# An attention and FFN kernel: a range check, two casts and a set of V loads take other places in the first two chunks

## The chip, the core and the metric

The kernel runs on one core of a Trainium2 chip. The metric is the device time of one execution in microseconds (us); less is better. The engines are TensorE (PE in the profile, with PEld for its weight loads), VectorE (DVE), ScalarE (ACT), GpSimd (POOL) and SyncE (SP). ACT, POOL and SP also issue DMAs. Each engine runs its instructions in the order in which the program gives them.

## The reference

Causal attention with a decay bias over 8 batches, 8 heads, 576 positions and head size 64, and behind it an FFN with RMS norm on the 4608 tokens:

```python
scores = scale * np.matmul(q, k.transpose(0, 1, 3, 2))
cum = np.cumsum(np.maximum(s, 0.0), axis=-1)
bias = -(cum[:, :, :, None] - cum[:, :, None, :])
scores = np.where(causal, -1000000000.0, scores + np.minimum(bias, 0.0))
attn = softmax(scores)                      # max subtracted, 1e-9 added to the sum
x = np.matmul(attn, v)                      # heads side by side: 4608 x 512
xn = x / np.sqrt(np.mean(x * x, axis=-1, keepdims=True) + 1e-06) * rms_g
g = xn @ w_gate                             # 512 x 1536
out = (g * sigmoid(g) * (xn @ w_val)) @ w_out
```

## The kernel before

**Attention by blocks.** Each batch has five blocks of positions (four of 128, one of 64). For a batch b the kernel does:

- load K and Q in float32 into `kq32` (w = 0 is K, w = 1 is Q; a main part with four row groups, and a tail), and cast them to bf16 into `kqn`, a row group at a time (`cast`, lines 139 and 141, and `cast_x`, line 149). `kqn` has two places, b % 2;
- transpose them into `kqT`. Batches 0 and 1 do it on PE (`t_step`, lines 184 to 192, and `tail_step`, lines 200 to 209); for batches 2 and 3 PE transposes K, and five DMAs of SP, c0 to c4, transpose Q (`kq_dma`, line 171); later batches use DMAs for both;
- S(b, kb, g), `s_step`: the scores of key block kb and four heads (g is 0 or 1; for kb = 4 all eight heads at once), matmuls at line 250, exponentials on ACT at line 274, and the causal mask on POOL at line 283 (`mask`);
- AV(b, qb, g), `av_step`: the value step of query block qb, matmuls at lines 300 and 306 with V in `v_sb`, and on DVE the reciprocal of the sums (line 313) and the product (line 315). After g = 1 come the sum of squares (DVE line 325 or ACT line 321) and, on POOL, its scale `al_all` (lines 328 and 331);
- `x_scale` on DVE (line 338), and a transpose into `xnT`, the input of the FFN: for batch 0 and for block 3 of batch 1 on PE (`xt_step`, line 357, copied at line 364 or 366), for the others by a DMA of SP (line 348).

V comes by DMAs that POOL issues, five per batch (`load_v`, line 175).

**The range check.** The kernel's fast path holds only for inputs within a range, so the largest magnitudes of Q and K are kept. `check_mag` (line 369, one DVE instruction of 128x2560) clears the signs into `mag`, and two `check_max` (line 375, 128x1280 each) take the running maximum into `acc`. It runs for K and Q of every batch.

**The order of work.** The program fixes the order by hand. A first part, written out instruction by instruction (lines 773 to 884), does nearly all of batch 0's attention. Then come nine FFN chunks of 512 tokens (`ffn`): 12 pairs of gate and value products (lines 668 and 677; T is ACT's tanh at line 671, U and Ht are DVE's products at lines 680 and 673), and then the output product in four blocks (line 690, copied by ACT at line 695, stored by SP at line 697). The matmuls of a chunk are cut by 36 calls of `step`, the slots; slots 1 to 36 lie in the first chunk, 37 to 72 in the second. A slot hands out the work of the coming batches: at most one entry of each side queue whose condition holds, then one score step, or value steps and transposes. `phase()` is the slot within its chunk, and slots with `bare` set skip the queue of V loads and the queue of POOL:

```python
bare = bare or chunk[0] == 0 and 30 <= phase() <= 33
if slot[0] % 2 and not bare:
    run_side(v_side)
if not bare:
    run_side(pool_side)
run_side(dve_side)
```

`later` puts functions into such a queue, due a number of slots from now; `early` does the same, and also keeps them to the first 23 slots of a chunk. `casts(b)` fills POOL's queue with the casts of batch b: five of Q, the mark `over(1)`, five of K, the mark `over(0)`. The mark `over(1)` lets Q's transposing DMAs start two slots later (at most one every second slot) and sets the loads of the next batch's Q four slots later. The mark `over(0)` lets K's transposes on PE start two slots later. A value step of batch 2 or above waits eight slots after the mark that V of its batch has been issued.

In the first chunk batch 0's last value step is in slot 10, batch 1's steps AV(1,2,1) and AV(1,3,1) are in slots 28 and 30, S(1,4) in slot 31, x_scale(1,2) and x_scale(1,3) in slots 31 and 33, and the PE transpose of block (1,3), which the second chunk needs, in slot 34. With the conditions of before, Q of batch 2 is cast by POOL in slots 24 to 28, V of batch 2 is loaded in slots 27, 29, 35, 37 and 39, `over(1)` is in slot 29, and K of batch 2 is cast in slots 34 to 38.

For the start of batch 1, ACT casts four row groups of its K in slots 1 to 4, POOL the tail in slot 1; DVE casts two row groups of its Q in slots 3 and 4, and POOL the other two and the tail in slots 4 to 6.

Of the kernel before, what the change touches and what calls it, by code (L numbers as in the profile page):

```python
# [26 lines left out]
def kernel(  # L27
# [12 lines left out]
    nc = tc.nc  # L40
# [63 lines left out]
    def psF16():  # L104
        return pp.tile([128, 8, 128], BF16, name="psF16", tag="F", bufs=4)
# [13 lines left out]
    def psT32():  # L119
        return pp.tile([128, 512], FP32, name="psT32", tag="T", bufs=1)  # L120
# [14 lines left out]
    def cast(eng, b, w, r0, r1, h0=0, h1=H):  # L135
        o = kqn[:, b % 2, w, r0:r1, h0:h1, :]
        i = kq32[:, w].rearrange("p h (r d) -> p r h d", d=D)[:, r0:r1, h0:h1, :]
        if eng is nc.scalar:
            eng.activation(out=o, in_=i, func=AF.Copy)
        else:  # L140
            eng.tensor_copy(out=o, in_=i)
# [52 lines left out]
    def tail_step(b):  # L194
        pT = psT()
        nw = 2 if b < XB else 1
        for w in range(nw):
            for hp in range(HP):
                i = w * HP + hp
                nc.tensor.matmul(  # L200
                    pT[:, i, :], lhsT=kqn[:, b % 2, w, 4, 2 * hp:2 * hp + 2, :],
                    rhs=ident_bf, is_transpose=True, start=(i == 0), stop=(i == nw * HP - 1))
        dst, src = kqTn[:, b % 2, 0, :, 512:576], pT[:, 0:HP, 0:64]
        if b == 0:
            nc.vector.tensor_copy(out=dst, in_=src)
        else:
            nc.scalar.activation(out=dst, in_=src, func=AF.Copy)
        if nw == 2:
            nc.vector.tensor_copy(out=kqTn[:, b % 2, 1, :, 512:576], in_=pT[:, HP:8, 0:64])
# [125 lines left out]
    def x_scale(b, qb):  # L335
        n = rows(qb)
        col = b * NSC + qb
        nc.vector.scalar_tensor_tensor(  # L338
            out=xs_sb[0:n, (b * NSC + qb) % NX, :], in0=x_sb[0:n, (b * NSC + qb) % NX, :],
            scalar=al_all[0:n, col:col + 1], in1=g_row[0:n], op0=ALU.mult, op1=ALU.mult)  # L340
# [32 lines left out]
    def check_max(i):  # L373
        sl = slice(i * 1280, (i + 1) * 1280)
        nc.vector.tensor_tensor(out=acc[:, sl], in0=acc[:, sl], in1=mag[:, sl], op=ALU.max)  # L375
# [27 lines left out]
    def run_side(queue):  # L403
        if queue and queue[0][0]():
            queue.pop(0)[1]()
            return True
        return False
# [21 lines left out]
    def phase():  # L429

        return slot[0] - first[0]
# [14 lines left out]
    def casts(b):  # L446

        def key(c):  # L450
            load_k(b, c)
            done["K", b, c] = slot[0]
            if c == NSC - 1:
                check(b)

        def over(w):
            done["cast", b, w] = slot[0]
            if b + 1 < B and (w == 1 or b + 1 < KB):
                loads(b + 1, w, early, 4)
            if w == 1:  # L460
                x_seq.extend((b, ww, c) for c in range(NSC) for ww in ((1, 0) if b >= KB else (1,)))
            else:
                done["cast", b] = slot[0]
                check(b)

        def free(w):
            return ready(0, "check", b - 2, w) and (
                ready(0, "T", b - 2) if w == 0 and b < KB + 2 else
                b < XB + 2 or ready(4, "X", b - 2, w, 4))
        if b >= KB:  # L470
            pool_side.extend((lambda: free(0) and slot[0] % 2 == 0, lambda c=c: key(c)) for c in range(NSC))
        fns = [(1, lambda r=r: cast_x(nc.gpsimd, b, 1, r)) for r in range(NSC)]
        fns += [(1, lambda: over(1))]
        if b < KB:
            fns += [(0, lambda r=r: cast(nc.gpsimd, b, 0, r, r + 1)) for r in range(NSC)]
            fns += [(0, lambda: over(0))]
        pool_side.extend((lambda w=w: ready(7, "raw", b, w) and free(w), f) for w, f in fns)

# [3 lines left out]

    def after_av(b):
        if b + 2 < B:
            (early if b else later)(v_side, 6 if b else 16, [
                lambda r=r: load_v(b + 2, r) for r in range(NSC)]
                + [lambda: done.__setitem__(("V", b + 2), slot[0])])

# [24 lines left out]
    def do_av(key, ps=None, act=False):  # L513
        b, qb, g = key
        act = act or b > 1 or b == 1 and qb > 1
        av_step(b, qb, g, ps, act)
        done["AV", b, qb, g] = slot[0]
        last["AV"] = slot[0]
        if b > 0 and g == 1:
            last["AVT"] = slot[0]  # L520
        if qb == 4 and g == 1:
            after_av(b)

    def do_xt(key, pX=None):
        b, qb = key
        xt_step(b, qb, pX)
        done["XT", b, qb] = slot[0]
        last["T"] = slot[0]
# [13 lines left out]
    def can_s():  # L542
        if not s_seq or not slot_free():
            return False
        b, kb, g = s_seq[0]
        if b == 1 and (phase() < 24 and phase() % 2 == 0 or kb == 4 and at("AV", 1, 3, 1) > slot[0]):
            return False
        due = SLOTS * ((b * S + kb * 128) // DM) - (26 if b == 1 else 18 if b < 4 else 14)
        if slot[0] - last["S"] < (4 if slot[0] < due - 24 else 3 if slot[0] < due else 2):
            return False  # L550
        if b >= XB:
            return all(ready(5, "X", b, 1, c) for c in (kb, min(kb + 1, 4))) and (
                ready(5, "X", b, 0, kb) if b >= KB else ready(3, "T", b) if kb >= 3 else
                all(ready(3, "T", b, hp, 0) for hp in (2 * g, 2 * g + 1)))
        if kb >= 3 and not ready(3, "T", b):
            return False
        if kb == 4:
            return True
        return all(ready(3, "T", b, 2 * g + j, w) for j in (0, 1) for w in (0, 1))
# [39 lines left out]
    def step(bare=False):  # L599

        slot[0] += 1
        while pending:
            pending.pop(0)()
        moved = False
        if scaled[0] < len(x_list):
            b, qb = x_list[scaled[0]]
            if ready(3, "AV", b, qb, 1):
                x_scale(b, qb)
                scaled[0] += 1
                if not by_pe(b, qb):  # L610
                    assert xt_seq[0] == (b, qb)
                    xt_dma(*xt_seq.pop(0))
                    done["XT", b, qb] = slot[0] + 4
                    moved = True
        run_side(act_side)
        if not moved and x_seq and slot[0] - last["X"] >= 2:
            b, w, c = x_seq[0]
            if (ready(2, "cast", b, 1) and ready(1, "S", b - 2, 4, 0)
                    and (w == 1 or ready(7, "K", b, c))):
                x_seq.pop(0)  # L620
                kq_dma(b, w, c)
                done["X", b, w, c] = last["X"] = slot[0]
                if b >= KB and (w, c) == (0, NSC - 1) and b + 2 < B:
                    casts(b + 2)
        bare = bare or chunk[0] == 0 and 30 <= phase() <= 33
        if slot[0] % 2 and not bare:
            run_side(v_side)
        if not bare:
            run_side(pool_side)
        run_side(dve_side)  # L630
        if can_s():
            pending.append(do_s(s_seq.pop(0)))
            if t_seq and t_seq[0][0] == 1 and can_t():
                do_t(t_seq.pop(0))
            return
        n = 0
        if can_xt():
            do_xt(xt_seq.pop(0))
            n += 1
        if can_av():  # L640
            do_av(av_seq.pop(0))
            n += 1
        if n < 2 and t_seq and can_t():
            do_t(t_seq.pop(0))
# [126 lines left out]
    with tc.manual_schedule():  # L771
# [31 lines left out]
        def pairF():  # L803
            return (psF(), psF())

        def s_first(kb, g, pair=None):
            do_s((0, kb, g), pair)()
# [31 lines left out]
        do_t((0, 2, 1), pT=psT(), dve=True)  # L839
        do_t((0, 3, 1), pT=psF16(), dve=True)  # L840
        do_av((0, 0, 0))
        s_first(0, 1, pairF())
        do_av((0, 1, 0), psT32())
        s_first(1, 1)
        tail_step(0)
        done["T", 0] = 0
        load_v(0, 4)
        do_av((0, 2, 0))
# [28 lines left out]
        do_xt((0, 2), psF16())  # L877
        warm(2)
        x_scale(0, 3)
        do_xt((0, 3), psF16())  # L880
        check_mag(0, 1)
        check_max(0)
        check_max(1)
        done["check", 0, 1] = 0

        def done_cast(w):
            done["cast", 1, w] = slot[0]
        later(act_side, 1, [lambda r=r: cast(ACT, 1, 0, r, r + 1) for r in range(4)])
        later(pool_side, 1, [lambda: cast(POOL, 1, 0, 4, 5)])
        later(pool_side, 3, [lambda: done_cast(0)])  # L890
        later(pool_side, 4, [lambda: cast(POOL, 1, 1, 2, 3),
# [207 lines left out]
```

## Time and profile before

| | us |
|---|---|
| median of 3 runs | 376.06 (375.62 to 376.51) |
| the profiled execution | 374.85 |
| its span, from the first to the last instruction | 373.2 |
| PE busy | 347.1 |
| DVE busy | 279.6 |
| ACT busy | 240.0 |
| POOL busy | 175.2 |

The mean granted clock of PE is 0.988. A line of the profile in order of time gives the start, the length, the engine, the line of the kernel, the operation, what it writes and reads, and how many instructions were merged; in brackets stand the engine's idle time ahead of it and what ended that idle time. `kq` stands for `kq32`. The first FFN matmul starts at 31.85, that of the second chunk at 76.10, and that of the third at 115.28.

### The profile page before, as it was taken

The numbers are of one execution on the slowest core, as the hardware profiler recorded it, in microseconds if no ns is written. First come the engines' busy times: TensorE is split into PE (matmuls) and PEld (weight loads), VectorE is DVE, ScalarE is ACT, GpSimd is POOL, SyncE is SP. The second block draws the span as 40 slices with busy tenths as digits, with TensorE's granted clock in tenths as the row PEclk, the third lists the DMA queues.
The fourth block names the chain that finished last, engine by engine and source line by source line (L and its number), as shares of the span: only waits on it lengthen the run. The fifth ranks groups of instructions, "written<-read, shape, count | busy, mean of one in ns | idle before, by whom it ended". The sixth has DMA issues, their size and how long they took to land. (4 is left out here: it accounts for less than half of the span.)

```text
span 373.2 us, 6936 instructions
## 1 busy us (share of the span) xinstructions
PE 347.1 (93%) x2356; PEld 161.4 (43%) x2356; DVE 279.6 (75%) x525; ACT 240.0 (64%) x626; POOL 175.2 (47%) x277
## 2 busy tenths in 40 slices
PE   1777899899999999899999999999999999999993
PEld 1443444454444444444444444444444444444441
DVE  6778988589887878788889897795488548837730
ACT  3787787547877597776778776777677644323321
POOL 5866734974846565779856825523322310000000
PEclk9879999999999999999999999999999999999998
DMA  7999999799997599959999997973310230020012
GB/s 228 192 206 262 148 208 210 122 201 222 127 204 104 52 200 161 159 56 204 147 166 223 139 118 151 122 56 44 99 23 14 44 105 3 0 84 31 0 42 78
DMA packets 125626, 46.22 MB, mean 124 GB/s; under 512 B 104912, under 2 KB 120784, under 8 KB 125584
## 3 DMA queue, kind: packets, MB, share of 16 engines
q0 software_dynamic: 59920, 11.80, 43.9%
q1 hardware_dynamic: 53040, 24.33, 34.7%
q10 hardware_dynamic: 12624, 9.59, 10.2%
q8 instruction: 20, 0.33, 0.4%
q14 instruction: 22, 0.18, 0.2%
HBM read 38.16 MB, written 9.44 MB: 128 GB/s over the span
## 5 line engine op out<-in xcount | busy, mean ns | idle before, releaser
L274 ACT ACTIVATE E<-psS,biasK 128x256 bf16<-128x256 f32 (+3 forms) x352 | 115.1, 416 | 19.7 <-PE psS L250 18.0
L668 PE MATMUL psF<-xnT,wg_sb 128*128 128x512 bf16 x432 | 111.1, 379 | 1.9 <-DMA xnT<-xs_sb 0.8
L677 PE MATMUL psF<-xnT,wv_sb 128*128 128x512 bf16 x432 | 111.1, 379 | 0.1
L690 PE MATMUL psF<-wout_sb,Ht 128*128 128x512 bf16 x432 | 102.3, 379 | 0.0
L283 POOL TENSOR_SCALAR_AFFINE_SELECT E<-E 128x512 bf16<-128x512 bf16 x72 | 51.9, 721 | 92.8 <-ACT E L274 92.0
L671 ACT ACTIVATE T<-psF 128x512 f32<-128x512 f32 x108 | 64.4, 598 | 41.5 <-PE psF L668 38.3
L680 DVE SCALAR_TENSOR_TENSOR U<-T,psF 128x512 bf16<-128x512 f32 x108 | 73.6, 682 | 21.8 <-ACT T L671 21.8
L673 DVE TENSOR_TENSOR Ht<-U,psF 128x512 bf16<-128x512 bf16 x99 | 67.7, 684 | 7.5 <-PE psS L250 0.5
L668 PEld LDWEIGHTS <-wg_sb 128*128 128x128 bf16 x432 | 38.7, 98 | 46.3 <-issue 7.5
L677 PEld LDWEIGHTS <-wv_sb 128*128 128x128 bf16 x432 | 38.6, 98 | 42.8 <-issue 4.6
L690 PEld LDWEIGHTS <-Ht 128*128 128x128 bf16 x432 | 38.7, 98 | 42.0 <-issue 2.3
L338 DVE SCALAR_TENSOR_TENSOR xs_sb<-x_sb,al_all,g_row 128x512 bf16<-128x512 bf16 (+1 forms) x40 | 32.4, 810 | 16.6 <-POOL al_all L331 15.0
L695 ACT ACTIVATE osb<-psF 128x512 f32<-128x512 f32 x36 | 21.4, 595 | 33.7 <-PE psF L690 29.3
L321 ACT ACTIVATE xs_sb<-x_sb 128x512 bf16<-128x512 bf16 (+1 forms) x36 | 22.9, 640 | 21.3 <-DVE x_sb L315 21.2
L175 POOL DMA_DIRECT2D v_sb<-in_v_dram x40 | 35.3, 883 | 0.4 <-issue 0.3
L375 DVE TENSOR_TENSOR acc<-acc,mag 128x1280 bf16<-128x1280 bf16 x32 | 29.5, 936 | 0.4
L250 PE MATMUL psS<-kqT 64*128 64x256 bf16 (+2 forms) x304 | 26.6, 260 | 1.4 <-ACT E L274 1.2
L306 PEld LDWEIGHTS <-E 128*128 128x128 bf16 x320 | 22.5, 99 | 12.1 <-POOL E L283 2.2
L328 POOL TENSOR_SCALAR al_all<-ss_all 128x1 f32<-128x1 f32 (+1 forms) x40 | 11.3, 282 | 27.6 <-ACT xs_sb L321 21.5
L300 PEld LDWEIGHTS <-E 128*128 128x128 bf16 x256 | 20.7, 99 | 8.0 <-DVE x_sb L315 0.8
L331 POOL TENSOR_TENSOR al_all<-al_all,mhalf 128x1 f32<-128x1 f32 (+1 forms) x40 | 22.6, 565 | 3.3
L250 PEld LDWEIGHTS <-kqT 64*128 64x128 bf16 x320 | 10.5, 96 | 29.9 <-issue 28.5
(94 smaller groups left out, 279.7 us busy)
## 6 DMA issues: line engine op xcount, KB each, us to landing
out_dram<-osb SPq DMA_DIRECT2D x36, 256.0 KB, 2.3
kq<-in_q_dram ACTq DMA_DIRECT2D x6, 1024.0 KB, 9.5
v_sb<-in_v_dram POOLq DMA_DIRECT2D x32, 128.0 KB, 7.2
kq<-in_k_dram ACTq DMA_DIRECT2D x2, 1024.0 KB, 10.6
kqn<-in_k_dram POOLq DMA_DIRECT2D x16, 128.0 KB, 4.9
wg_sb<-in_moe_w_gate_dram POOLq DMA_DIRECT2D x2, 768.0 KB, 7.3
wv_sb<-in_moe_w_val_dram POOLq DMA_DIRECT2D x2, 768.0 KB, 10.1
wout_sb<-in_moe_w_out_dram POOLq DMA_DIRECT2D x1, 1536.0 KB, 14.1
```

The source lines that it names most:

```text
L175: nc.gpsimd.dma_start(out=v_sb[0:n, b % 2, c, :, 0:64], in_=v[b, :, c * 128:c * 128 + n, :].rearrange("h p d -> p h d"))
L250: nc.tensor.matmul(pair[par][:, j * W:j * W + M], lhsT=kT, rhs=qT, start=(j == 0), stop=(j == nj - 1))
L274: nc.scalar.activation(out=eo, in_=ei, func=AF.Exp, scale=0.125, bias=biasK[:, kb, bh:bh + 1])
L283: nc.gpsimd.affine_select(out=Ev[:, :, 0:nq], in_=Ev[:, :, 0:nq], pattern=[[0, nh], [1, nq]], compare_op=ALU.is_ge, fill=0.0, base=0, chan ...
L338: nc.vector.scalar_tensor_tensor(out=xs_sb[0:n, (b * NSC + qb) % NX, :], in0=x_sb[0:n, (b * NSC + qb) % NX, :], scalar=al_all[0:n, col:col ...
L375: nc.vector.tensor_tensor(out=acc[:, sl], in0=acc[:, sl], in1=mag[:, sl], op=ALU.max)
L668: nc.tensor.matmul(Gp, lhsT=wg_sb[:, cc, fs], rhs=xnT[:, cc, x0:x0 + DM], start=(cc == 0), stop=(cc == CC - 1))
L671: nc.scalar.activation(out=T, in_=Gp, func=AF.Tanh, scale=0.5)
L673: nc.vector.tensor_tensor(out=Ht[:, fb - 1, :], in0=pend[0], in1=pend[1], op=ALU.mult)
L677: nc.tensor.matmul(Vp, lhsT=wv_sb[:, cc, fs], rhs=xnT[:, cc, x0:x0 + DM], start=(cc == 0), stop=(cc == CC - 1))
L680: nc.vector.scalar_tensor_tensor(out=U, in0=T, scalar=1.0, in1=Gp, op0=ALU.add, op1=ALU.mult)
L690: nc.tensor.matmul(Op, lhsT=Ht[:, fb, tb * 128:(tb + 1) * 128], rhs=wout_sb[:, fb, :], start=(fb == 0), stop=(fb == FB - 1))
```

## The change

Five edits, all in the first two chunks or ahead of them:

- the check of batch 0's Q (three DVE instructions) stood at the end of the first part; it is now cut up among the value steps of batch 0 there: `check_mag` behind AV(0,0,0), one `check_max` behind AV(0,1,0), the other behind the tail's transposes;
- two of the four K casts of batch 1 go from ACT (slots 3 and 4) to DVE, ahead of the last transpose of the first part;
- V of batch 2 is due 24 slots after batch 0's last value step instead of 16;
- the slots that skip the queues of V and POOL are 29 to 33 of the first chunk, instead of 30 to 33;
- the first of the K casts of batch 2 goes from POOL's queue to DVE, in slot 33.

```diff
@@ casts(b)
-            fns += [(0, lambda r=r: cast(nc.gpsimd, b, 0, r, r + 1)) for r in range(NSC)]
+            fns += [(0, lambda r=r: cast(nc.gpsimd, b, 0, r, r + 1)) for r in range(b == 2, NSC)]
@@ after_av(b)
-            (early if b else later)(v_side, 6 if b else 16, [
+            (early if b else later)(v_side, 6 if b else 24, [
@@ step()
-        bare = bare or chunk[0] == 0 and 30 <= phase() <= 33
+        bare = bare or chunk[0] == 0 and 29 <= phase() <= 33
...
         run_side(dve_side)
+        if slot[0] == 33:
+            cast(nc.vector, 2, 0, 0, 1)
@@ the first part
         do_av((0, 0, 0))
+        check_mag(0, 1)
         s_first(0, 1, pairF())
         do_av((0, 1, 0), psT32())
+        check_max(0)
         s_first(1, 1)
         tail_step(0)
+        check_max(1)
         done["T", 0] = 0
...
         x_scale(0, 3)
+        cast(DVE, 1, 0, 2, 3)
+        cast(DVE, 1, 0, 3, 4)
         do_xt((0, 3), psF16())
-        check_mag(0, 1)
-        check_max(0)
-        check_max(1)
         done["check", 0, 1] = 0
...
-        later(act_side, 1, [lambda r=r: cast(ACT, 1, 0, r, r + 1) for r in range(4)])
+        later(act_side, 1, [lambda r=r: cast(ACT, 1, 0, r, r + 1) for r in range(2)])
```

## The prediction

> **What bounds the kernel now.** I read the page first: TensorE (PE) carries the span.
>
> ```profile
> PE 347.1 (93%) x2356; PEld 161.4 (43%) x2356; DVE 279.6 (75%) x525; ACT 240.0 (64%) x626; POOL 175.2 (47%) x277
> ```
>
> So only PE's holes can give time. I listed PE in order of time for every idle gap. Before the first FFN matmul (31.85) PE waits for others all the time; after it four holes over 0.4 remain in front of the closing stage: 1.14, 0.48, 1.50, and 0.78 at 154.84 (an xnT transfer, which no edit touches). The first three:
>
> ```profile
> 36.50 0.33 PE L184 MATMUL psT<-ident_bf,kqn 128*128 128x128 bf16 x3
> 37.97 0.23 PE L184 MATMUL psT<-ident_bf,kqn 128*128 128x128 bf16 x1 [1.14 <-ACT kqn L139]
> ...
> 40.80 0.23 PE L184 MATMUL psT<-ident_bf,kqn 128*128 128x128 bf16 x1 [0.48 <-POOL kqn L141]
> ...
> 73.90 0.40 PE L357 MATMUL psT<-ident_bf,xs_sb 128*128 128x128 bf16 x4 [1.50 <-DVE xs_sb L338]
> ```
>
> Then DVE in order of time, for where the check of Q goes and what it leaves (last bracket: idle before, and its releaser):
>
> ```profile
> 17.15 0.42 DVE L315 TENSOR_TENSOR x_sb<-psAV,rZ 128x256 bf16<-128x256 f32 x1
> 18.06 0.18 DVE L313 RECIPROCAL rZ<-psT 128x4 f32<-128x4 f32 x1 [0.49 <-PE psT L306]
> ...
> 19.90 0.29 DVE L205 COPY kqT<-psT 128x256 bf16<-128x256 bf16 x1 [1.20 <-PE psT L200]
> ...
> 22.53 1.17 DVE L325 SCALAR_TENSOR_TENSOR xs_sb<-x_sb 128x512 bf16<-128x512 bf16 x1
> ...
> 30.63 1.47 DVE L369 TENSOR_SCALAR mag<-kqn 128x2560 uint16<-128x2560 uint16 x1
> 32.14 1.97 DVE L375 TENSOR_TENSOR acc<-acc,mag 128x1280 bf16<-128x1280 bf16 x2
> ```
>
> ACT and POOL around the first two holes: a K cast of ACT sits ahead of the eight exponentials of S(0,4), POOL's mask waits for those, and the Q casts that PE wants wait for the mask.
>
> ```profile
> 35.13 0.62 ACT L139 ACTIVATE kqn<-kq 128x512 bf16<-128x512 f32 x1
> 35.66 1.74 ACT L274 ACTIVATE E<-psS,biasK 128x64 bf16<-128x64 f32 x8
> 37.23 0.69 ACT L139 ACTIVATE kqn<-kq 128x512 bf16<-128x512 f32 x1
> ```
>
> ```profile
> 37.47 0.66 POOL L283 TENSOR_SCALAR_AFFINE_SELECT E<-E 128x512 bf16<-128x512 bf16 x1 [3.21 <-ACT E L274]
> 38.09 1.18 POOL L141 CAST kqn<-kq 128x512 bf16<-128x512 f32 x1
> 39.22 0.90 POOL L175 DMA_DIRECT2D v_sb<-in_v_dram  x1
> 40.12 1.78 POOL L141 CAST kqn<-kq 128x512 bf16<-128x512 f32 x2
> ...
> 70.03 0.19 POOL L328 TENSOR_SCALAR al_all<-ss_all 128x1 f32<-128x1 f32 x1
> 70.30 0.56 POOL L331 TENSOR_TENSOR al_all<-al_all,mhalf 128x1 f32<-128x1 f32 x1
> 70.82 0.95 POOL L175 DMA_DIRECT2D v_sb<-in_v_dram  x1
> 71.84 0.18 POOL L328 TENSOR_SCALAR al_all<-ss_all 128x1 f32<-128x1 f32 x1
> 72.11 0.57 POOL L331 TENSOR_TENSOR al_all<-al_all,mhalf 128x1 f32<-128x1 f32 x1
> ```
>
> The last lines are the third hole: the scale of block (1,3) stands behind a V load's issue.
>
> **A, the check between the value steps.** Three DVE instructions come into 17.57 to 22.53, where DVE idles 0.49 + 1.20 + 0.87 = 2.56 us. Alone they take 0.82 each (median of 16 and of 32), 2.46 in all, but the order is fixed. The first reads Q's tail, cast by POOL until 17.77, so it runs 17.83 to 18.65; behind it the reciprocal of AV(0,1,0) starts at 18.65 instead of 18.06, its product ends 0.56 late, and the tail transposes, which want its PSUM tile, start 0.56 late (19.41). The first max fills their 1.01 us. The second stands ahead of AV(0,2,0)'s reciprocal: after the tail copies (20.95) it ends at 21.8, that product near 22.4, AV(0,0,1)'s near 23.1, and the square (1.17) near 24.3 instead of 23.71: 0.55 late. POOL's scale of block (0,0), both last masks and the other three scales follow without a gap to spare, and so do the four transposes to xnT and the first FFN matmul. With the durations seen beside POOL work (1.11 for the mag at 37.70, 1.32 for a max at 40.11) it is 1.4. I take +0.8, since a mask (0.63) meets both maxes. At the old place nothing returns: the check held U(0) back 0.53 (34.04 against T's end 33.51), but PE's buffers had 0.8 to 1.4 us of slack there.
>
> The mag at 30.63 took 1.47, beside POOL's issue at 30.71, against 0.82 alone. The Trainium skill ("SBUF — State Buffer", section "Who interferes with whom") says that a DVE tensor_scalar in a two-port mode, or one with two SBUF inputs against a POOL instruction that reads, locks a shared port pair, and whoever comes second waits fully. By it each max waits out its mask and A is about +0.85; without it +0.55, and the whole sum -1.35 instead of -1.1.
>
> **B, two K casts from ACT to DVE.** DVE runs them (0.42 each) from x_scale(0,3)'s end, 30.71, where the check was. K landed at 23.88 + 5.5 = 29.4; both move with A, so the data is there 1.3 us early. If it were not, U(0) would wait, with the slack above. ACT loses 0.62 and 0.69: the exponentials start right after T(1) (35.24) and end at 36.88 instead of 37.40, and the 1.14 hole closes. But the next wait is the second hole's: POOL's mask and Q casts start 0.52 earlier, so the Q cast that PE waits for ends at 40.2 instead of 40.73, and PE, 1.14 early, waits there. Gain 0.52, not 1.62; 0.25 if DVE's mag of K again holds POOL (the 1.18 cast), 1.0 if it no longer does. I take -0.5.
>
> **C, POOL clear of V.** V of batch 2 moves from slots 27, 29, 35, 37, 39 to 35, 37, 39, 41, 43. Without the first two issues (0.95 each) Q's casts end near 69.0, block (1,2)'s scale runs 69.1 to 69.9, and block (1,3)'s starts when ACT's square is read (70.06): 0.19 + 0.56, then x_scale 0.75, at 71.7. PE is free for its transpose at 72.40: the 1.50 goes, or all but 0.2 if rows beside other work hold (0.80 for L328, 1.13 for x_scale). I take -1.4. Next late would be block (1,2)'s transfer to xnT: issued near 70.7, 3.6 to land (the row of before), 74.3; the next chunk then begins at 74.7. If it lands like the slowest nearby (4.6), 0.6 comes back.
>
> **Edits that go together at nothing.** The K cast on DVE in slot 33 (0.42) lies in DVE's idle 0.49 and 1.54 after x_scale(1,3); uncovered it delays an xnT copy that has 1.35 to spare. POOL then casts four rows in slots 35 to 38, and K of batch 2 is marked in slot 39 as before, so its transposes start in slot 41 as before. AV(2,0,0) goes from slot 51 to 54, since V is marked in 45 instead of 41: the same matmuls later in a busy PE. The load of Q's tail for batch 4 would fall on slot 60, where such loads are barred until the next chunk, and slips from 59 to 73; its casts slip only from 79 to 80.
>
> One move has a price: slot 29 is now barred to POOL's queue, so the mark "Q of batch 2 cast" waits until 34, and its five transposing DMAs go from slots 32 to 40 to slots 36 to 44, behind an output store. The second (c1) is issued near 77.2 instead of 74.97, and S(2,0,0) needs it at 85.85 - 1.4 = 84.4. Landings were 3.0 and 5.8 for the first two, and for the three issued beside the 1 MB load of Q (77.25):
>
> ```profile
> DMA to landing us min/median/max: 9.3/9.4/9.7
> ```
>
> Beside Q's load of batch 5, c0 and c1 landed in 6.7 and 5.4. I take 7, as those start with little queued like here: 84.2, just in time. Bounds 0 and +2.3.
>
> **Sum:** +0.8 - 0.5 - 1.4 = -1.1 on the profiled 374.85 (span 373.2 and 1.65 around it). That execution lies 1.21 under the median 376.06; on the median, 375.0.
>
> **Rivals.** *1. Q's transposes of batch 2 arrive late (slower).* In-order PE stops at S(2,0,0). For it: three of five landings above are 9.3 or more, when V and Q's load ran too, as they now do. Against: batch 5's. At 9.4, c1 lands at 86.6, 2.2 too late: -1.1 + 2.2 = +1.1, 377.2. It costs from a landing of 7.2 us on; the sign turns at 8.3, and at 9.05 the kernel is slower by 0.2%. The Trainium skill ("DMA: Bandwidth & Descriptors", section "Queues, rings and completion order") says that each DMA engine serves its queues in turn, packet by packet; by it three busy queues (SP, ACT, POOL's V) stretch c1 as they did at 77 to 81, and the trace agrees with 9.4 there against 5.4 with two. Chance 0.2.
>
> *2. The check is dearer and POOL stays the bound.* A +1.4 and B -0.25 (contention rows), C -1.3: -0.15, 375.9. For it: DVE leaves hardly a gap after 21.86. Chance 0.2.
>
> *3. Everything hides well.* A +0.55, B -1.0, C -1.5: -1.95, 374.1. For it: POOL is idle 17.77 to 19.12, when the mag runs. Chance 0.15.
>
> **Numbers.** Forecast, -1.1 and no late transfer: 0.45, faster. Rival 3 is faster, rival 2 the same, rival 1 slower in 0.15 and the same in 0.05. Faster by over 0.2% (0.75 us, about what a measurement of this kernel can tell from no change) 0.60, within it 0.25, slower 0.15. The range goes from 373.6 (rival 3, with the next chunk's holes of 0.38 at 93.03 and 0.17 at 101.12 closed too) to 377.0 (rival 1 at a landing of 9.2).
>
> **What would show it.** Right: the first FFN matmul 0.8 later; the 1.14 hole gone, a wait for POOL's Q cast near 40 of about 1 us; no hole ahead of block (1,3)'s transpose, with al_all of (1,3) right behind ACT's square; V's issues after it. Wrong: a first FFN matmul no later or over 1.4 later; a hole in front of S(2,0,0) waiting for kqT; one at the next chunk's first matmul waiting for xnT.

## The result: slower by half a per cent, and the profile after

| | median us (lowest to highest, runs) |
|---|---|
| before | 375.86 (375.19 to 377.09, 13) |
| changed | 377.65 (376.20 to 380.44, 13) |
| ratio, 95% interval | 1.0055 (1.0038 to 1.0071) |

The forecast was 375.0, faster; the change lies outside the range, on the side of rival 1 (377.2). Its profiled execution took 380.44 with a span of 378.8 and is the slowest of its 13 runs: PE's granted clock was 0.54 from 33 to 36, which cost chunk 1 about 1.7. A second profile of the same kernel (span 375.2) does not have this dip, and the profile of run 5, whose first part is that of before, has it (0.55). So where sizes are compared below, that second profile is used too. It is the fastest of its six runs (376.93 to 379.95), so it shows the loss at its small end.

PE in order of time, in the changed kernel; the lines answer to the three holes of before:

```profile
40.71 0.33 PE L184 MATMUL psT<-ident_bf,kqn 128*128 128x128 bf16 x3
42.59 0.23 PE L184 MATMUL psT<-ident_bf,kqn 128*128 128x128 bf16 x1 [1.54 <-POOL kqn L141]
...
74.03 0.39 PE L357 MATMUL psT<-ident_bf,xs_sb 128*128 128x128 bf16 x4
...
85.01 1.03 PE L679 MATMUL psF<-xnT,wv_sb 128*128 128x512 bf16 x4
88.44 0.39 PE L250 MATMUL psS<-kqT 64*128 64x256 bf16 x4 [2.40 <-DMA kqT<-kqn]
```

The holes of 1.14 and 0.48 have become one of 1.54. The hole of 1.50 ahead of block (1,3)'s transpose is gone. A new one of 2.40 stands ahead of S(2,0,0), which waits for a transposing DMA. POOL, in order of time, shows why the third hole went: both scales now come ahead of V's issues.

```profile
70.85 0.19 POOL L328 TENSOR_SCALAR al_all<-ss_all 128x1 f32<-128x1 f32 x1
71.13 0.55 POOL L331 TENSOR_TENSOR al_all<-al_all,mhalf 128x1 f32<-128x1 f32 x1
71.93 0.58 POOL L328 TENSOR_SCALAR al_all<-ss_all 128x1 f32<-128x1 f32 x1 [0.26 <-ACT xs_sb L321]
72.60 0.55 POOL L331 TENSOR_TENSOR al_all<-al_all,mhalf 128x1 f32<-128x1 f32 x1
73.56 0.89 POOL L283 TENSOR_SCALAR_AFFINE_SELECT E<-E 128x512 bf16<-128x512 bf16 x1 [0.41 <-ACT E L274]
74.40 0.95 POOL L175 DMA_DIRECT2D v_sb<-in_v_dram  x1
75.36 1.17 POOL L141 CAST kqn<-kq 128x512 bf16<-128x512 f32 x2
76.47 0.89 POOL L175 DMA_DIRECT2D v_sb<-in_v_dram  x1
```

The issues of SP and ACT, in order of time, show what the first two transposes (c0, c1) now run beside: V's two issues above, and the 1 MB load of Q, issued 0.09 behind c0.

```profile
77.28 5.05 SPq L171 DMA_TRANSPOSE kqT<-kqn  x3
77.37 0.40 ACTq L125 DMA_DIRECT2D kq<-in_q_dram  x1
```

And the landing of c0 and c1, and who waited for them (view of the transposes' line, issues from 77 to 80):

```profile
L171 SPq DMA_TRANSPOSE kqT<-kqn x2: 1430/1734/2037, 77.3 to 78.8; - x2
...
  PE psS L250: 2.4, 1
...
DMA to landing us min/median/max: 9.5/9.5/9.6
```

Before, they were issued at 72.96 and 74.97, ahead of the same load (77.25), and landed in 3.0 and 5.8. Issues in order of time, before (at 77.16 start the other three transposes, those that landed in 9.3 to 9.7):

```profile
72.96 1.23 SPq L171 DMA_TRANSPOSE kqT<-kqn  x1
...
74.26 0.95 POOL L175 DMA_DIRECT2D v_sb<-in_v_dram  x1
...
74.97 1.22 SPq L171 DMA_TRANSPOSE kqT<-kqn  x1
...
76.33 0.89 POOL L175 DMA_DIRECT2D v_sb<-in_v_dram  x1
...
77.16 4.65 SPq L171 DMA_TRANSPOSE kqT<-kqn  x3
77.25 0.39 ACTq L125 DMA_DIRECT2D kq<-in_q_dram  x1
```

Two of V's loads are issued in slots 35 and 37 in both kernels, 74.26 and 76.33 here and 74.40 and 76.47 after. What is new for c0 and c1 is their own later time, beside the load of Q and behind those two.

A chunk is measured here from its first FFN matmul to the next chunk's; in these rows the work of PE in a chunk hardly changes (38.6 to 38.9 busy in chunk 2), so a longer chunk is a chunk with holes.

| kernel | first FFN matmul | chunk 1 | chunk 2 | chunks 3 and 4 |
|---|---|---|---|---|
| before | 31.85 | 44.25 | 39.18 | 77.95 |
| changed | 32.21 | 44.01 | 43.10 | 78.80 |
| changed, second profile | 32.49 | 42.33 | 41.55 | 78.22 |

Chunk 1 gave 1.92 and chunk 2 took 2.37 back in the second profile, 0.64 was lost ahead of chunk 1 and 0.27 behind chunk 2. By chunk 5's start that is +1.36; the spans differ by 2.0, and the rest lies in the closing stage, whose length differed by some 0.6 between executions of kernels that were edited nowhere near it.

### The profile page after: what moved, and what is told of

Its sections match the earlier page's. It is cut to its first block, busy times and chain, and to the rows that moved or that the text cites. A ratio compares the mean times of both kernels' runs of the same rounds, so it can differ in the third digit from the quotient of the medians.

```text
span 378.8 us, 6937 instructions
## 1 busy us (share of the span) xinstructions
PE 348.8 (92%) x2356; PEld 161.8 (43%) x2356; DVE 280.3 (74%) x528; ACT 238.8 (63%) x624; POOL 175.8 (46%) x276
## 5 line engine op out<-in xcount | busy, mean ns | idle before, releaser
L283 POOL TENSOR_SCALAR_AFFINE_SELECT E<-E 128x512 bf16<-128x512 bf16 x72 | 54.4, 756 | 94.6 <-ACT E L274 94.0
L670 PEld LDWEIGHTS <-wg_sb 128*128 128x128 bf16 x432 | 38.9, 98 | 47.3 <-issue 9.0
L679 PEld LDWEIGHTS <-wv_sb 128*128 128x128 bf16 x432 | 38.9, 98 | 43.6 <-issue 5.7
L375 DVE TENSOR_TENSOR acc<-acc,mag 128x1280 bf16<-128x1280 bf16 x32 | 27.9, 884 | 0.3
## 6 DMA issues: line engine op xcount, KB each, us to landing
v_sb<-in_v_dram POOLq DMA_DIRECT2D x32, 128.0 KB, 10.2
```

What stands on the lines that cost most here:

```text
L283: nc.gpsimd.affine_select(out=Ev[:, :, 0:nq], in_=Ev[:, :, 0:nq], pattern=[[0, nh], [1, nq]], compare_op=ALU.is_ge, fill=0.0, base=0, chan ...
L670: nc.tensor.matmul(Gp, lhsT=wg_sb[:, cc, fs], rhs=xnT[:, cc, x0:x0 + DM], start=(cc == 0), stop=(cc == CC - 1))
L679: nc.tensor.matmul(Vp, lhsT=wv_sb[:, cc, fs], rhs=xnT[:, cc, x0:x0 + DM], start=(cc == 0), stop=(cc == CC - 1))
```

## The experiments

Three theories stood at the start. **T1:** the late mark `over(1)` sends c0 and c1 off beside Q's load, and PE waits for c1 at S(2,0,0). **T2:** PE's granted clock falls in the first chunk. **T3:** V's later loads crowd POOL or the DMA engines, whatever the mark does.

Runs 1 to 4, 5 to 8 and 9 to 12 were timed on one chip each, beside the kernel before, whose median was 375.24, 375.95 and 375.56 there; a ratio is to that one, with its 95% interval.

**1. The changed kernel again** (no edit).

> The changed kernel once more, for a second profiled execution. Theory T1 (the transposing DMAs c0 and c1 of batch 2's Q, held back by the mark over(1), land late): the hole in front of S(2,0,0), 2.40 us in the first profiled execution, is there again, between 1.5 and 3. Theory T2 (TensorE's granted clock falls in the first FFN chunk because the first part is laid out anew): the clock is 0.5 again for some 3 us from 32 on, and the first FFN matmul group takes about 1.7 instead of 1.02. Theory T3 (V's later loads crowd the DMA engines): besides that hole, the hole at the start of chunk 4 (waiting for xnT) is over 1.5 again instead of 0.78. Time 1.5 to 2 over the kernel before.

Measured: 378.14, ratio 1.0081 (1.0053 to 1.0109). The clock holds at full speed through chunk 1, and the hole is there:

```profile
86.47 0.40 PE L250 MATMUL psS<-kqT 64*128 64x256 bf16 x4 [1.84 <-DMA kqT<-kqn]
```

T2 falls: the dip does not come with the new first part. In the chunks PE's clock drops to about half in four of the fourteen profiles, those of the changed kernel, of run 5 (0.55 from 33 to 36), of run 7 (0.51 from 88 to 91, behind the hole) and of run 6 (0.50 from 161 to 167, behind a hole of 4.39). Whether a hole of PE makes such a dip likelier is not shown: behind the holes of 2.40, 1.84 and 2.60 there is none.

**2. The mark put back to slot 29; all else changed.**

```diff
-        bare = bare or chunk[0] == 0 and 29 <= phase() <= 33
+        bare = bare or chunk[0] == 0 and 30 <= phase() <= 33
```

> The changed kernel, but slot 29 is open to POOL's queue again, so that the mark over(1) falls in slot 29 as in the kernel before; V of batch 2 stays in slots 35 to 43, the other edits stay too. T1: the hole in front of S(2,0,0) goes, 2.4 us come back, and the time is 0.5 to 1.5 under the kernel before. T3: the hole stays at over 1 us, since V's five loads still fall beside Q's, and the time stays over the kernel before. T2: nothing changes but by chance.

Measured: 374.84, ratio 0.9988 (0.9961 to 1.0015). c0 and c1 are issued at 72.31 and 74.25, land in 2.7 and 8.4, and there is no hole ahead of S(2,0,0). Against run 1 that is 0.9% back, so the late mark carries the loss. But chunk 2 still lasts 40.89, 1.7 more than before: 1.2 more in holes (of 0.17 to 0.72, which wait for ACT's kqT and E and for POOL's mask), and the rest because more of PE's work falls into the chunk (39.11 busy against 38.63). T1 is right and not the whole.

**3. Only the late V, the barred slot 29 and the K cast in slot 33**, no check moved and no cast of batch 1 moved.

> The kernel before with only the three edits around slots 27 to 43: slot 29 barred, V of batch 2 due 24 slots after, the first K cast of batch 2 on DVE in slot 33. Check and K casts of batch 1 as before. T1: the hole of 1.50 ahead of block (1,3)'s transpose goes and one of 2 to 3 in front of S(2,0,0) comes, so 0.5 to 1.5 slower than before. T2: the clock stays at 1.0 from 31 on and the time is at or under the kernel before.

Measured: 376.93, ratio 1.0040 (1.0022 to 1.0057). Chunk 1 is 42.57, so C is worth 44.25 - 42.57 = 1.68. Chunk 2 is 42.20, with 2.60 ahead of S(2,0,0). The gain and the loss both come with these three edits.

**4. Only the check and the two K casts.**

> The kernel before with only the check moved between the value steps and the two K casts on DVE. My sum: first FFN matmul 0.36 to 0.8 later, 0.5 gained in the two holes near 37 and 40: within 0.5 of the kernel before. T2: the clock falls to 0.5 near 32 and the time is 1 to 2 over the kernel before. T1: no hole in front of S(2,0,0), and the hole of 1.50 ahead of block (1,3) stays.

Measured: 375.77, ratio 1.0012 (0.9997 to 1.0028): no difference that can be told, and chunk 2 as before (39.17). From the first FFN matmul to the end of the second hole it has 40.88 - 32.18 = 8.70 where before has 8.95: B gives 0.25. POOL's mask is what holds it, beside DVE's mag:

```profile
37.27 1.20 POOL L283 TENSOR_SCALAR_AFFINE_SELECT E<-E 128x512 bf16<-128x512 bf16 x1 [3.01 <-ACT E L274]
38.44 0.60 POOL L141 CAST kqn<-kq 128x512 bf16<-128x512 f32 x1
```

**5. Only V later; 6. only slot 29 barred.**

```diff
-            (early if b else later)(v_side, 6 if b else 16, [
+            (early if b else later)(v_side, 6 if b else 24, [
```

> The kernel before, with only V of batch 2 moved later (slots 35 to 43); the mark behind Q's casts then falls in slot 29, all K casts stay on GpSimd, no check is moved. If only the late transposes of Q cost the change its gain: no hole ahead of S(2,0,0), chunk 1 shorter by 1.5 to 1.7 and chunk 2 as long as before: 1.5 below the kernel before. If V's later loads themselves crowd the DMA engines or GpSimd in chunk 2: chunk 2 longer by 1.2 to 1.7 as when the mark was put back early, and the time within 0.5 of before. If it was the K cast on VectorE in slot 33 that lengthened chunk 2 there: chunk 2 as before here.

Measured: 376.06, ratio 1.0011 (0.9982 to 1.0039). No hole ahead of S(2,0,0) (c0 and c1 land in 2.7 and 8.6, in time), the hole of 1.50 is gone, and chunk 2 lasts 40.91, about what run 2 had, without the K cast on DVE. The waits are others than there: 0.49 and 0.50 for DVE's U and 0.77 for xnT at the start of chunk 3. So late V costs chunk 2 about 1.7 on its own: T3 holds beside T1, and the cast in slot 33 is not needed for it. Chunk 1 is 43.70 and not 42.6 to 42.8 as expected, since this profile has the dip of the clock in it.

> The kernel before, with only slot 29 barred to GpSimd's queue, so that the mark behind Q's casts waits until slot 34 and V's second issue until 35; its first stays in 27. If the late mark alone makes the transposes late: PE idles 1.5 to 2.5 ahead of S(2,0,0) for kqT, chunk 2 is 2 to 3 longer, chunk 1 is 0.5 to 1.0 shorter, and the time is 0.8 to 2 above before. If the lateness needs V's later loads beside it: no hole over 0.5 there, and the time 0.5 to 1 below before.

Measured: 385.73, ratio 1.0254 (1.0221 to 1.0286), far from both expectations. With five K casts left to POOL behind slot 33, `over(0)` and all that is written by slots behind it moves too, and chunks 2 to 5 are each 2.7 to 4.5 longer; this run does not isolate the mark. Of the 4.5 of chunk 3, 4.39 is one wait for xnT at the start of chunk 4; what made that transfer late was not followed up. One reading of it counts: with V's first load back in slot 27, and two more in slots 35 and 37 as in the kernel before, c0 landed in 9.3 and c1 in 8.4 all the same. So it is not the change's move of V that puts V's loads beside them. This time PE lost 1.94 in another way, through ACT. ACT's K load is held until c0 lands (76.49 + 9.3), and with it the copy that PE waits for:

```profile
85.89 0.38 ACTq L125 DMA_DIRECT2D kq<-in_k_dram  x1
86.31 0.60 ACT L192 ACTIVATE kqT<-psT 128x512 bf16<-128x512 bf16 x1 [3.58 <-DMA kqT<-kqn]
```

**7. The changed kernel with that K load four slots later**, to see whether ACT's wait costs anything there.

```diff
-                loads(b + 1, w, early, 4)
+                loads(b + 1, w, early, 4 if b != 2 or w else 8)
```

> The changed kernel with one line more: the K load of batch 3, which ScalarE issues and which waits there for the landing of Q's first transpose, four slots later. If that wait on ScalarE costs time of its own, its idle of 2.9 to 3.3 ahead of T goes and chunk 2 is 0.5 to 1.2 shorter than in the changed kernel. If TensorE's own wait for the second transpose covers it, the hole ahead of S(2,0,0) stays near 2 and chunk 2 stays within 0.3 of the changed kernel's 41.6 to 43.1.

Measured: 377.88, ratio 1.0049 (1.0023 to 1.0075), as the changed kernel; chunk 2 is 42.23. The load no longer holds ACT (issued at 88.17), but ACT still idles 2.40, now because PE stands still, and the hole ahead of S(2,0,0) is 2.00. At that place PE's own wait covers ACT's. Whether the rest of chunk 2 is shorter cannot be told from this profile: the clock dip behind the hole made PE busy for 40.06 where the second profile of the changed kernel has 38.83. Without those 1.23 the chunk would be near 41.0 against 41.55 (an estimate).

**8. V earlier, in slots 17 to 25.**

```diff
-            (early if b else later)(v_side, 6 if b else 16, [
+            (early if b else later)(v_side, 6 if b else 6, [
```

> The kernel before, with V of batch 2 moved earlier instead of later, to slots 17 to 25, where GpSimd idles; nothing else changed. If GpSimd's order ahead of block (1,3) is the whole hole of 1.50 and V's late loads are what lengthens chunk 2: hole gone, chunk 1 shorter by 1.3 to 1.7, chunk 2 as before or shorter, 373.5 to 374 where before has 375.2. If five more transfers beside the 1 MB loads of Q and K delay Q's casts by as much: no gain or up to 1 us lost.

Measured: 375.13, ratio 0.9984 (0.9960 to 1.0008). Chunk 2 is 39.18, as before; chunk 1 is 43.48, with 0.88 left of the hole, since an issue of V (65.12 to 65.87) still stands among Q's casts (run 11 bears that out). The gain is about half of what was expected, and the interval reaches no change.

**9 and 10. The changed kernel, without one of the two neighbours of c0 and c1.** In run 9 the 1 MB load of Q goes seven slots later; in run 10 V goes to slots 13 to 21 (lag 2).

```diff
-                loads(b + 1, w, early, 4)
+                loads(b + 1, w, early, 4 if b != 2 or not w else 11)
```

> The changed kernel with the 1 MB load of Q of batch 3, issued 0.1 us behind the first late transpose, put seven slots later; later loads of that queue slip with it. If that load is what stretches the first two transposes from 3.0 and 5.8 to over 9: they land in 4 to 7, the hole ahead of S(2,0,0) shrinks from 1.8 to 2.4 to under 0.5 and chunk 2 is 1.5 to 2 shorter up to there; what the delayed loads cost afterwards is not part of it. If V's five loads stretch them: landing stays over 8.5 and the hole over 1.2.

Measured: 375.43, ratio 0.9995 (0.9977 to 1.0012). The transposes, issued at 75.4 and 76.7, late as in the changed kernel, and with V's loads at 72.47 and 74.54 ahead of them:

```profile
L171 SPq DMA_TRANSPOSE kqT<-kqn x2: 1240/1272/1303, 75.4 to 76.7; - x2
...
DMA to landing us min/median/max: 3.7/4.2/4.6
```

No hole, and chunk 2 lasts 39.26: not only the 1.84 to 2.40 are gone, but also the 1.7 that late V cost in runs 2 and 5. The time is still that of before, since chunks 3 and 4 take 79.18 instead of 77.95, with a wait of 1.70 ahead of chunk 4.

> The changed kernel with V of batch 2 put early (slots 13 to 21) instead of late; the mark stays in slot 34, the transposes behind it, and Q's load beside them. If V's loads stretch the transposes: c0 and c1 land in 4 to 7 and no hole over 0.5 stands ahead of S(2,0,0); the time is then 1 to 2.5 below the changed kernel. If the mark's lateness with Q's load is enough: landing over 8.5, the hole stays 1.2 to 2.4 and the time within 1 of the changed kernel.

Measured: 374.28, ratio 0.9970 (0.9951 to 0.9989). With the load of Q beside them, 0.09 behind c0, but V long landed:

```profile
L171 SPq DMA_TRANSPOSE kqT<-kqn x2: 1402/1490/1577, 75.3 to 76.7; - x2
...
DMA to landing us min/median/max: 5.3/5.9/6.5
...
83.93 0.39 PE L250 MATMUL psS<-kqT 64*128 64x256 bf16 x4
```

No hole; chunk 2 lasts 38.63, chunk 1 42.33. The load of Q itself lands in 6.2 instead of 10.2 and that of K behind it in 7.0 instead of 14.8. The output store that SP issues ahead of c0 stands there in both runs (74.94 and 74.82), so it is not what makes them late. Either neighbour alone leaves the transposes in time; both together make them late. That is the cause, shown from both sides.

**11 and 12. Better kernels.** Run 11 is the kernel before with V in slots 13 to 21 and nothing else; run 12 adds the two K casts on DVE and leaves the check at its old place.

```diff
-            (early if b else later)(v_side, 6 if b else 16, [
+            (early if b else later)(v_side, 6 if b else 2, [
...
+        cast(DVE, 1, 0, 2, 3)
+        cast(DVE, 1, 0, 3, 4)
...
-        later(act_side, 1, [lambda r=r: cast(ACT, 1, 0, r, r + 1) for r in range(4)])
+        later(act_side, 1, [lambda r=r: cast(ACT, 1, 0, r, r + 1) for r in range(2)])
```

> The kernel before with V of batch 2 in slots 13 to 21, four slots earlier than when it was put in 17 to 25: there GpSimd still had a V issue (0.75) between Q's casts and a hole of 0.88 stayed ahead of block (1,3). If that issue is the rest of the hole: under 0.4 now, chunk 1 at 42.9 or less against 44.25, chunk 2 as before, 1.0 to 1.5 below the kernel before. If the hole's rest is VectorE's scale running 1.12 beside GpSimd's mask: hole stays 0.5 to 0.9 and the gain 0.6 to 0.8.

> V of batch 2 in slots 13 to 21 and the two K casts on VectorE, the check left at its old place behind them. If each part keeps what it gave alone: first FFN matmul as before (31.4 to 31.9), 1.14 hole gone with 0.9 to 1.3 left of the two holes by 41, 0.25 to 0.5 more than V alone, 1.3 to 2 below the kernel before. If the check behind the casts holds U(0), that hole comes back as a wait for VectorE near 34 of 0.3 to 1.

Measured: 373.68, ratio 0.9946 (0.9934 to 0.9959), and 373.06, ratio 0.9932 (0.9917 to 0.9947). Both beat the kernel before and the changed one. The third hole is gone in both, the transposes go out in slot 32 as before, and chunk 2 is 39.18 in both. In run 12 the first two holes come to 0.57 + 0.61 = 1.18 instead of 1.62:

```profile
38.85 1.02 PE L668 MATMUL psF<-xnT,wg_sb 128*128 128x512 bf16 x4 [0.57 <-DVE Ht L673]
40.66 0.23 PE L184 MATMUL psT<-ident_bf,kqn 128*128 128x128 bf16 x1 [0.61 <-POOL kqn L141]
...
72.27 0.39 PE L357 MATMUL psT<-ident_bf,xs_sb 128*128 128x128 bf16 x4
```

Run 11 gained 0.4 and run 12 0.5 us more than the top of what was expected. The wait for DVE came, not near 34 but at 38.85. The two intervals overlap, so what the casts add to early V is not settled.

## Why the prediction was wrong

**The step that failed is the price of the move of `over(1)`:** "I take 7, as those start with little queued like here: 84.2, just in time. Bounds 0 and +2.3." Landing of the two was 8.9 to 9.8 in four profiles with the late mark and late V (the changed kernel twice, runs 3 and 7). The rest of that step was near: in the second profile c1 was issued at 77.4 and PE was ready for S(2,0,0) at 86.47 - 1.84 = 84.63, against 77.2 and 84.4 forecast. The reason given was wrong by the rows at hand. Q's load stood at 77.25 before, 75.85 with the forecast 1.4 taken off, and c1 at 77.2 puts c0 a little ahead of that (75.88 in the second profile, the load at 75.96): the transposes were being moved from ahead of that load to the same moment, with two of V's loads, those of slots 35 and 37, just under way. The three rows at 9.3 to 9.7, issued beside that load and behind those loads of V, were the near neighbours. Batch 5's two were not: V's loads come there behind them, the first 2.20 after c0 and 0.46 after c1 (132.35):

```profile
130.61 4.32 SPq L171 DMA_TRANSPOSE kqT<-kqn  x3
...
132.81 1.84 POOL L175 DMA_DIRECT2D v_sb<-in_v_dram  x2
```

So rival 1 was wrong to set batch 5's 5.4 down to two queues: V's loads ran beside that transpose too, for most of its time. Rival 1 had the mechanism, the place and the price (2.2 against 1.84 to 2.60), and its chance of 0.2 was too low. The range left that price out: its upper end, 377.0, took a landing of 9.2, below the rows of 9.3 to 9.7.

The Trainium skill ("DMA: Bandwidth & Descriptors", section "Queues, rings and completion order") lets each DMA engine serve its queues in turn; by it three busy queues stretch a transpose and two do less. The runs agree: 9.5 with SP, ACT's load and V; 4.6 and 3.7 without ACT's load; 6.5 and 5.3 without V. How many queues are busy does not settle the time alone, as batch 5's 6.7 and 5.4 show.

**A cost that was not in the sum:** V's lateness itself. "The same matmuls later in a busy PE" was true of AV(2,0,0), but V's loads in slots 35 to 43 land in 4.6 to 16.7 (median 13.7, changed kernel) among Q's and K's loads, and chunk 2 grows by 1.7 with the transposes in time (runs 2 and 5). This and the late transposes do not add up: with both, chunk 2 grew by 2.37 in the second profile and by 3.02 in run 3. Run 9 points to the meeting of V with ACT's loads here too: V stays late there, Q's load and those behind it come later, and the cost is gone.

**C was right and a little small:** 1.68 against 1.4. The hole closed wholly, with the scale right behind ACT's square and V's issues behind it, as the prediction said these rows would look.

**B was over-sized:** 0.25 against 0.5, its lower bound, and by the reason given for that bound. The 1.14 hole went and POOL's Q cast became the wait, 1.54 long; POOL's mask took 1.19 to 1.20 beside DVE's mag instead of 0.66.

**A was over-sized:** seven profiles with the check moved start the FFN at 31.86 to 32.53 (mean 32.24), seven without at 31.39 to 32.18 (mean 31.87; run 12 belongs there): +0.37 against 0.8, below the lower bound of 0.55. Counted from the product of AV(0,0,0), which leaves out what came before, it is 14.72 to 15.12 (mean 14.93) against 14.24 to 14.70 (mean 14.55), much the same. DVE in order of time, after:

```profile
17.68 0.83 DVE L369 TENSOR_SCALAR mag<-kqn 128x2560 uint16<-128x2560 uint16 x1
18.43 0.17 DVE L313 RECIPROCAL rZ<-psT 128x4 f32<-128x4 f32 x1
...
18.98 0.81 DVE L375 TENSOR_TENSOR acc<-acc,mag 128x1280 bf16<-128x1280 bf16 x1
...
20.66 0.81 DVE L375 TENSOR_TENSOR acc<-acc,mag 128x1280 bf16<-128x1280 bf16 x1
21.39 0.17 DVE L313 RECIPROCAL rZ<-psAV 128x4 f32<-128x4 f32 x1
```

The next instruction starts 0.73 to 0.75 behind the first and the last of these three, not 0.82, and the chain from AV(0,0,0)'s product to the square is 22.88 - 17.29 = 5.59 where it was 22.53 - 17.15 = 5.38. Here the maxes did not wait for POOL's masks; it was the other way round, because DVE started first:

```profile
19.26 1.02 POOL L283 TENSOR_SCALAR_AFFINE_SELECT E<-E 128x512 bf16<-128x512 bf16 x1 [1.61 <-ACT E L274]
20.72 1.25 POOL L283 TENSOR_SCALAR_AFFINE_SELECT E<-E 128x512 bf16<-128x512 bf16 x1 [0.43 <-ACT E L274]
```

These masks took 0.63 and 0.64 before. In three of the seven profiles (runs 2, 7 and 10) the second mask came first, by 0.15, and there the max was the long one, as the prediction had it. In run 2, POOL and then DVE:

```profile
20.74 0.64 POOL L283 TENSOR_SCALAR_AFFINE_SELECT E<-E 128x512 bf16<-128x512 bf16 x1 [0.22 <-ACT E L274]
...
20.89 1.17 DVE L375 TENSOR_TENSOR acc<-acc,mag 128x1280 bf16<-128x1280 bf16 x1
```

The chain from that product to the square is 5.87 to 5.88 in these three, and 5.39 to 5.60 in the other four. The Trainium skill ("SBUF — State Buffer", section "Who interferes with whom") says that the second to come waits; the traces agree with that, and the term of 0.85 that the prediction drew from it was too large because it took DVE to be second at both maxes.

**The edits at nothing:** the K cast in slot 33 showed no cost in chunks 1 and 2 (run 10 has it and the shortest chunk 2). One wait grew that nobody moved: ahead of chunk 4 PE stands for 1.14 and 1.70 in the changed kernel's two profiles, against 0.78 before, mostly until an xnT transfer lands. It is 1.14 to 1.73 in all seven profiles with the K cast in slot 33 and 1.29 in run 12, which has not got it; run 6 apart (4.39), the others have 0 to 0.78. Part of it is given back in chunk 4, and chunks 3 and 4 together are 0.3 to 1.2 longer in those eight. What causes it was not settled, and the cast is not cleared of it.

Together, in the second profile: -1.92 in chunk 1 (C and B: 1.68 + 0.25) as forecast, and +2.37 in chunk 2, 1.84 of it the hole, where the forecast had nothing.

## What to carry to other kernels

When an edit shifts a mark, follow every DMA that the mark releases to its new time and ask what else is issued in that microsecond; a landing time belongs to its neighbours, so take it from the row with the same neighbours, those already under way above all, not from the row with the same queue length. Work that must leave a crowded stretch is better moved ahead of it than behind it: V later cost 1.7 and more, and V earlier, into POOL's idle time, kept the whole gain. And a wait that was hidden by time in hand needs its own row in the sum when the time in hand falls to nothing.

## What the runs showed of the hardware that was not expected

- The landing of a transpose of one size depends on its company: the same two transposes took 3.0 and 5.8 ahead of the load, 4.6 and 3.7 beside V alone, 6.5 and 5.3 beside the 1 MB load alone, and 8.4 to 9.8 beside both (runs 3, 6 and 7 and the changed kernel). Both are not always that dear: batch 5's two, with V's loads issued behind them, took 6.7 and 5.4.
- An engine that issues a load can be stopped by a transfer that has nothing to do with it. ACT's K load came out about 0.1 behind the landing of one of Q's transposes in nine profiles, among them: c0 in the changed kernel (77.28 + 9.5, load at 86.87), its second profile (84.9, 84.94), runs 3, 6 and 10 (85.2, 85.32; 85.8, 85.89; 81.8, 81.84), and c1 in runs 2 and 5 (82.65, 82.77; 83.98, 84.07). In the traces the DMAs of SP and ACT take eight completion semaphores in turn, and none starts before the DMA that had its semaphore last has landed. In the changed kernel c0 and the K load have the same one, with seven other issues between them. ACT stood still for 3.33 in the changed kernel and for 3.58 in run 6, where it stopped PE.
- Of a DVE check instruction and a POOL mask, the one that started second was the long one: masks of 1.02 to 1.25 instead of 0.63 behind DVE's 0.81 to 0.83, and a max of 1.17 behind a mask of 0.64.
